# Attention and gated feed-forward on one core: the first pair's queries and first three key blocks come in fp32 by the hardware queues, and GpSimd's cast loads wait for those keys

## The chip, the cores and the metric

The kernel runs on one core of a Trainium2 chip. The metric is the device time of one execution in microseconds (us). The profile is that of one execution; its span is counted from the first to the last instruction.

## The reference

Attention over 8 batches of 8 heads with 1152 positions of 64 elements, in which neighbouring queries are averaged in pairs (1152 queries become 576), and behind it a feed-forward without a nonlinearity: two projections are multiplied element by element, then come two more matrices.

```
q_pool = q.reshape(B, H, S // 2, 2, D).mean(axis=3)
scores = matmul(q_pool, k.T) / sqrt(D)
attn   = softmax(scores)                  # over the 1152 keys
x      = (attn @ v) as [B * 576, 512]     # heads side by side
out    = ((x @ w1) * (x @ w2)) @ w3 @ w_out
```

Inputs and output are fp32; `w1`, `w2` are 512x1024, `w3` 1024x1024, `w_out` 1024x512; the output is 4608x512.

## The kernel before

All matrix work is done in fp16 with fp32 sums. Two heads are one *pair*: there are 32 pairs, and a pair has 9 key blocks of 128 keys. In a pair the two heads' queries lie on the two halves of the 128 partitions once they are transposed.

**Loads.** `load_q`, `load_k` and `load_v` (lines 75 to 97) issue from GpSimd's queue; they read fp32 from memory and write fp16 into the staging tiles `qst`, `kst` and `vst`, so each is a cast load. `load(P)` issues keys, queries and values of a pair. GpSimd also issues the weights (`load_w3`, `load_ffn`, `load_wo`, lines 313 to 331). Lines 430 to 443 write out the order of the first loads by hand: queries of pair 0, its keys in two pieces (blocks 0 to 2, then 3 to 8), the identity for the transposes (`memset` and `affine_select`), values of pair 0, then pair 1, a quarter of `w3`, pair 2, `w_out`, another quarter, pair 3, a third. Later loads are issued from inside the main loop. GpSimd takes them strictly in this order, and at most eight of its DMAs are in flight: the ninth waits for the first to land, through a semaphore that they share.

**The first pair.** `prep_first` (lines 171 to 199) makes the operands of pair 0. ACT copies key blocks 0 to 2 from `kst` to `kc` (line 179). VectorE adds neighbouring queries in two pieces, blocks 0 to 3 and 4 to 8 (line 183; the factor of one half is in the scale of the exponential). TensorE transposes queries (line 189) and keys (line 168) against the identity, VectorE copies the transposed queries to `qT` (line 192), ACT the keys to `kT` (line 197). Key blocks 3 to 8 follow in `prep_rest` (lines 201 to 208), behind the first three chunks of scores. For pairs 1 to 7, VectorE adds the queries (`pool_q`, line 121) and copies the keys (line 164), TensorE transposes both in one group and VectorE takes them out (lines 224 to 232). From pair 8 on GpSimd adds the queries, and the SP queue transposes by DMA (`prep_dma`).

**The main loop** (lines 505 to 562). The scores of all pairs are one stream of chunks of 512 columns. `scores` (line 253) writes a chunk for both heads into a PSUM tile `psc` of three buffers, which the transposes and half of the side work share; `expo` (line 263) takes it through the exponential on ACT into the ring `er`, which holds 9216 columns (18 chunks) for each head. `attend` (line 278) multiplies the ring's columns with the values. How many such products follow in each of the 108 iterations stands in the list `PVS`. Between them TensorE works off a queue of side work: transposing `w3` (line 343), multiplying it with `w_out` into `T16` (line 355), and early feed-forward groups (lines 371 and 389). VectorE empties the PSUM tiles of that work (lines 348, 359, 381, 383) in the program's order, in which its copies for the next pair stand too. What is left of the feed-forward comes after the loop.

**Names that the steps below touch.** `seen` is a tile of one element, which the helper `settled` (line 151) fills on GpSimd with a copy of one element of `kT`, so that GpSimd waits for what wrote it. `ident` is the identity. Each engine runs its instructions in the order in which the program issues them.

Of the kernel before, what the change touches and what calls it, by code (L numbers as in the profile page):

```python
# [7 lines left out]
FP32 = mybir.dt.float32  # L8
# [7 lines left out]
NJ = 9  # L16
PAIR = SQ * NJ
CH = 512
RING = 9216
# [4 lines left out]
def kernel(  # L24
# [11 lines left out]
    nc = tc.nc  # L36
    B, H, S, D = q.shape
# [23 lines left out]
    er = const.tile([128, 2, RING], FP16)  # L61
# [3 lines left out]
    seen = const.tile([1, 1], FP16)  # L65
# [7 lines left out]
    kst, vst, qst, kT, qT, kTs, qTs, qps = {}, {}, {}, {}, {}, {}, {}, {}  # L73

    def load_q(P):
        b, h0 = P // 4, 2 * (P % 4)
        if P % 2 == 0:
            qst[P // 2] = stage.tile([128, 2, 18, D], FP16, tag="qst", bufs=2, name="qst")
        o = 64 * (P % 2)
        nc.gpsimd.dma_start(  # L80
            out=qst[P // 2][o:o + 64].rearrange("p u t d -> p u (t d)"),
            in_=q[b, h0:h0 + 2].rearrange("u (p t) d -> p u (t d)", t=18))

    def load_k(P):
        b, h0 = P // 4, 2 * (P % 4)
        kst[P] = stage.tile([128, 2, NJ, D], FP16, tag="kst", name="kst")
        for js in ((0, 3), (3, NJ)) if P == 0 else ((0, NJ),):
            nc.gpsimd.dma_start(  # L88
                out=kst[P][:, :, js[0]:js[1], :],
                in_=k[b, h0:h0 + 2].rearrange("u (p j) d -> p u j d", j=NJ)[:, :, js[0]:js[1], :])  # L90

    def load_v(P):
        b, h0 = P // 4, 2 * (P % 4)
        vst[P] = stage.tile([128, 2, NJ, D], FP16, tag="vst", name="vst")
        nc.gpsimd.dma_start(  # L95
            out=vst[P].rearrange("p u j d -> p u (j d)"),
            in_=v[b, h0:h0 + 2].rearrange("u (p j) d -> p u (j d)", j=NJ))

    def load(P):
        if P < NP:  # L100
            load_k(P)
            load_q(P)
            load_v(P)

    def load_two(P):
        load_q(P)
        load_q(P + 1)
        load_v(P)
        load_v(P + 1)
        load_k(P)  # L110
        load_k(P + 1)
# [13 lines left out]
    def new_kq(P):  # L125
        if P % 2 == 0:
            kTs[P // 2] = ab.tile([128, 2, NJ, 128], FP16, tag="kT", bufs=2, name="kT")
            qTs[P // 2] = ab.tile([128, NJ, 128], FP16, tag="qT", bufs=2, name="qT")
        o = 64 * (P % 2)
        kT[P] = kTs[P // 2][:, P % 2]  # L130
        qT[P] = qTs[P // 2][:, :, o:o + 64]
# [23 lines left out]
    def new_kc(P):  # L155
        if P % 2 == 0:
            kc2[P // 2] = ab.tile([128, 2, NJ, 2, D], FP16, tag="kc", bufs=1, name="kc")
        kcs[P] = kc2[P // 2][:, P % 2]
        return kcs[P]
# [6 lines left out]
    def keys(P, dst, js):  # L166
        for n, j in enumerate(js):
            nc.tensor.transpose(dst[:, 128 * n:128 * n + 128],
                                kcs[P][:, j].rearrange("p u d -> p (u d)"), ident)

    def prep_first():

        new_kq(0)
        kc = new_kc(0)
        qp = qps[0] = ab.tile([128, NJ, 2, D], FP16, tag="qp", bufs=2, name="qp")
        src = qst[0][0:64].rearrange("p u (c two) d -> p u c two d", two=2)
        tq = psum.tile([128, 2, 1024], FP16, tag="psc", bufs=3, name="tq")
        tk = psum.tile([128, 2, 1024], FP16, tag="psc", bufs=3, name="tk")
        nc.scalar.copy(out=kc[:, 0:3].rearrange("p j u d -> p u j d"), in_=kst[0][:, :, 0:3])
        parts = (range(0, 4), range(4, NJ))  # L180
        for cs in parts:
            r = slice(cs[0], cs[-1] + 1)
            nc.vector.tensor_tensor(
                out=qp[0:64, r].rearrange("p c u d -> p u c d"),
                in0=src[:, :, r, 0, :], in1=src[:, :, r, 1, :], op=ALU.add)
        for h, cs in enumerate(parts):
            for c in cs:
                o = 64 * (c - cs[0])
                nc.tensor.transpose(tq[:, h, o:o + 64],
                                    qp[0:64, c].rearrange("p u d -> p (u d)"),  # L190
                                    ident[0:64, 0:64])
            nc.vector.tensor_copy(
                out=qT[0][:, cs[0]:cs[-1] + 1],
                in_=tq[:, h, 0:64 * len(cs)].rearrange("p (c f) -> p c f", f=64))
            if h == 0:
                keys(0, tk[:, 0], range(0, 3))
                nc.scalar.copy(out=kT[0][:, 0:3].rearrange("p j f -> p (j f)"),
                               in_=tk[:, 0, 0:384])
        return tk
# [162 lines left out]
    def ffn_groups(t):  # L362
# [64 lines left out]
    NIT = NCHUNK // BURST  # L427
    NPV = NP * 90

    load_q(0)  # L430
    load_k(0)
    nc.gpsimd.memset(ident, 0.0)
    nc.gpsimd.affine_select(
        out=ident, in_=ident, compare_op=ALU.not_equal, fill=1.0,
        base=0, channel_multiplier=1, pattern=[[-1, 128]])
    load_v(0)
    load(1)
    load_w3(0)
# [4 lines left out]
    load_w3(2)  # L443
    loaded, staged, prepped, copied = 4, 1, 1, 1
    rest = prep_first()

    n_units = NT // 512
# [41 lines left out]
    for c in range(NF):  # L489
        t = (6, 7, 8, 9, 11, 12, 14, 15)[c]  # L490
# [115 lines left out]
```

## Time and profile before

| | us |
|---|---|
| four runs | 422.08, 422.26, 423.63, 426.41 |
| median | 422.94 |
| profiled execution, whole time | 423.63 |
| its span | 421.9 |
| TensorE (PE) matmuls busy | 404.1 (96% of the span) |
| ScalarE (ACT) busy | 326.3 (77%) |
| VectorE (DVE) busy | 198.0 (47%) |
| GpSimd (POOL) busy | 121.0 (29%) |
| GpSimd's DMA queue | 33.56 MB written, 51.5% of 16 engines' span |
| SP's DMA queue | 24.66 MB, 32.7% |

Lines with `PE` are matmuls and transposes, with `PEld` the loading of their stationary operand. In a timeline line stand: start, length, engine, line of the kernel, operation, tile written and tile read, shapes, count, and in brackets the idle time before with what ended it. A cast load is counted by the bytes that it writes, half of those that it reads. GpSimd is busy while it issues a DMA; the transfer itself runs on the 16 DMA engines.

### The profile page before, as it was taken

How to read it: one execution, taken by the hardware profiler on the slowest of the kernel's cores; microseconds unless marked ns; L12 is line 12 of the kernel's file. 1: busy time of each engine (PE TensorE's matmuls, PEld its weight loads, DVE VectorE, ACT ScalarE, POOL GpSimd, SP SyncE). 2: the span in 40 equal slices, each digit the busy share in tenths (PEclk: the TensorE clock that was granted, in tenths of full speed). 3: DMA queues.
4: the chain of work that ended last, by engine and by line, in shares of the span. 5: the costliest groups of instructions: out<-in, count | busy, mean ns of one | idle time of the engine just before them, and what ended most of it. 6: DMA issues, size and time to landing. Idle time of an engine off the chain costs nothing.

```text
span 421.9 us, 12560 instructions
## 1 busy us (share of the span) xinstructions
PE 404.1 (96%) x5432; PEld 268.2 (64%) x5432; DVE 198.0 (47%) x406; ACT 326.3 (77%) x355; POOL 121.0 (29%) x160
## 2 busy tenths in 40 slices
PE   3998999999999999999999999999999999999995
PEld 1576778666685568665865686667765876544443
DVE  1455655564535543545445535544457434714130
ACT  4899899889888889889888889888888889133332
POOL 8323332253434343423316161524243000000000
PEclk9999999999999999999999999999999999999999
DMA  8999999778989989998989898989899650050404
GB/s 123 202 208 204 180 193 176 122 138 145 156 154 174 184 148 184 170 143 122 165 127 174 148 183 131 206 131 172 164 174 130 113 114 18 13 117 0 102 0 100
DMA packets 94729, 59.15 MB, mean 140 GB/s; under 512 B 65361, under 2 KB 85073, under 8 KB 94673
## 3 DMA queue, kind: packets, MB, share of 16 engines
q0 software_dynamic: 26544, 33.56, 51.5%
q1 hardware_dynamic: 67968, 24.66, 32.7%
q8 instruction: 42, 0.69, 0.7%
q10 hardware_dynamic: 160, 0.13, 0.1%
q14 instruction: 15, 0.11, 0.1%
HBM read 67.11 MB, written 9.44 MB: 181 GB/s over the span
## 4 chain that ended last, share of the span: by engine, by line
PE 79%; DMA 16%; DVE 2%; POOL 1%; issue 1%; ACT 0%; SPq 0%; DVEq 0%; POOLq 0%
PE po L278 18%; PE psc L253 16%; PE pa L371 15%; PE pb L371 15%; PE pp L389 15%; DMA qst<-in_q_dram 7%; DMA w3h<-in_moe_w_dram 4%; DMA w1sb<-in_moe_w_dram 4%; PE pT L355 1%; DMA out_dram<-osb 1%; DVE vt L134 1%; POOL kst L88 1%; DVE gT L383 0%; POOL vst L95 0%; POOL qst L80 0%
## 5 line engine op out<-in xcount | busy, mean ns | idle before, releaser
L263 ACT ACTIVATE er<-psc 128x1024 f16<-128x1024 f32 x324 | 307.7, 1026 | 44.6 <-PE psc L253 44.3
L278 PEld LDWEIGHTS <-er 128*128 128x128 f16 x2880 | 103.9, 98 | 23.7 <-issue 7.0
L278 PE MATMUL po<-vt,er 128*128 128x65 f16 x2880 | 111.3, 194 | 0.7 <-DVE xn L295 0.4
L253 PE MATMUL psc<-qT,kT 64*128 64x512 f16 (+7 forms) x1152 | 97.3, 290 | 6.0 <-ACT er L263 2.8
L383 DVE TENSOR_TENSOR gT<-pb,asb 128x512 f16<-128x512 f32 x72 | 49.8, 692 | 55.8 <-PE pb L371 55.0
L371 PE MATMUL pa<-xT,w1sb 128*128 128x512 f16 x288 | 74.2, 380 | 0.0
L371 PE MATMUL pb<-xT,w2sb 128*128 128x512 f16 x288 | 74.1, 380 | 0.0
L389 PE MATMUL pp<-T,gT 128*128 128x256 f16 (+1 forms) x488 | 67.9, 292 | 0.0
L253 PEld LDWEIGHTS <-kT 64*128 64x128 f16 x1152 | 46.4, 95 | 31.1 <-issue 11.0
L389 PEld LDWEIGHTS <-gT 128*128 128x128 f16 x488 | 45.6, 98 | 18.5 <-issue 3.7
L381 DVE COPY asb<-pa 128x512 f32<-128x512 f32 x56 | 38.7, 691 | 39.0 <-PE pa L371 37.8
L371 PEld LDWEIGHTS <-w2sb 128*128 128x128 f16 x288 | 26.4, 98 | 32.7 <-issue 3.9
L371 PEld LDWEIGHTS <-w1sb 128*128 128x128 f16 x288 | 25.0, 98 | 30.1 <-issue 6.2
L121 POOL TENSOR_TENSOR qp<-qst 128x1152 f16<-128x1152 f16 x12 | 28.5, 2375 | 48.2 <-DMA qst<-in_q_dram 26.4
L401 DVE TENSOR_SCALAR osb<-pp 128x256 f32<-128x256 f32 x49 | 20.8, 425 | 39.3 <-PE pp L389 32.6
L291 DVE RECIPROCAL rz<-po 128x5 f32<-128x5 f32 x64 | 12.4, 193 | 47.2 <-PE po L278 46.7
L295 DVE TENSOR_TENSOR xn<-po,rz 128x320 f16<-128x320 f32 x64 | 31.5, 492 | 2.2
L141 POOL COPY kc<-kst 128x576 int32<-128x576 int32 x24 | 15.9, 666 | 51.3 <-DMA kst<-in_k_dram 51.3
L95 POOL DMA_DIRECT2D vst<-in_v_dram x32 | 23.5, 745 | 13.2 <-DMA kst<-in_k_dram 4.0
L88 POOL DMA_DIRECT2D kst<-in_k_dram x33 | 24.1, 743 | 8.4 <-DVE rz L291 2.6
L398 ACT ACTIVATE osb<-pp 128x512 f32<-128x512 f32 (+1 forms) x12 | 7.0, 579 | 24.2 <-PE pp L389 23.1
L80 POOL DMA_DIRECT2D qst<-in_q_dram x32 | 19.9, 624 | 13.0 <-issue 3.1
(39 smaller groups left out, 127.8 us busy)
## 6 DMA issues: line engine op xcount, KB each, us to landing
qst<-in_q_dram POOLq DMA_DIRECT2D x32, 288.0 KB, 6.5
vst<-in_v_dram POOLq DMA_DIRECT2D x32, 288.0 KB, 10.0
out_dram<-osb SPq DMA_DIRECT2D x70, 128.0 KB, 2.6
kst<-in_k_dram POOLq DMA_DIRECT2D x31, 288.0 KB, 12.3
w3h<-in_moe_w_dram POOLq DMA_DIRECT2D x4, 512.0 KB, 15.8
xT<-in_moe_w_out_dram POOLq DMA_DIRECT2D x2, 512.0 KB, 14.6
w1sb<-in_moe_w_dram POOLq DMA_DIRECT2D x2, 512.0 KB, 16.2
w2sb<-in_moe_w_dram POOLq DMA_DIRECT2D x2, 512.0 KB, 17.7
```

The source lines that it names most:

```text
L88: nc.gpsimd.dma_start(out=kst[P][:, :, js[0]:js[1], :], in_=k[b, h0:h0 + 2].rearrange("u (p j) d -> p u j d", j=NJ)[:, :, js[0]:js[1], :])
L95: nc.gpsimd.dma_start(out=vst[P].rearrange("p u j d -> p u (j d)"), in_=v[b, h0:h0 + 2].rearrange("u (p j) d -> p u (j d)", j=NJ))
L121: eng.tensor_tensor(out=qps[pp][r].rearrange("p c u d -> p u c d"), in0=src[:, :, :, 0, :], in1=src[:, :, :, 1, :], op=ALU.add)
L253: nc.tensor.matmul(t[:, u, o:o + ln].rearrange("p (c f) -> p c f", f=64), kT[P][s, j, :], qT[P][s, f0 // 64:(f0 + ln) // 64], start=True, ...
L263: nc.scalar.activation(out=er[:, :, r:r + CH], in_=psc.pop(c), func=AF.Exp, bias=0.0, scale=SCALE)
L278: nc.tensor.matmul(po[P, u][:, VW * x:VW * x + D + 1], er[:, u, r:r + 128], vts[P % 4][:, u, j, 0:D + 1], start=(m == 0), stop=(m == 44), ...
L295: nc.vector.tensor_tensor(out=xn[:, P % 2, :, u, :], in0=acc[:, :, 0:D], in1=rz.to_broadcast([128, 5, D]), op=ALU.mult)
L371: nc.tensor.matmul(p, w[:, mc, ft * 128:ft * 128 + 128], xT[:, mc, t0:t0 + 512], start=(mc == 0), stop=(mc == NC - 1))
L381: nc.vector.tensor_copy(out=asb[ft], in_=p)
L383: nc.vector.tensor_mul(out=gT[:, ft, :], in0=p, in1=asb.pop(ft))
L389: nc.tensor.matmul(p[:, 0:n], gT[:, ft, 128 * i:128 * i + 128], T16[:, ft, n * s:n * s + n], start=(ft == 0), stop=(ft == NF - 1))
L401: nc.vector.tensor_scalar_mul(out=osb, in0=p[:, 0:n], scalar1=1.0 / (SCL * SCL))
```

## The change

`load_first` issues three DMAs at the program's head: from SP the queries of pair 0, in two pieces (8 and 10 of the 18 consecutive rows that each of 64 partitions holds for a head), and from ACT its key blocks 0 to 2. They are fp32 without a cast, and land in the end of the exponentials' ring `er`, whose columns are seen as fp32 (`q0f`, `k0f`); the ring's end is first written by the exponentials of chunks 9 to 17. `prep_first` reads the queries and keys from there: VectorE's two adds and ACT's copy now have fp32 operands. GpSimd's two cast loads of the same data are gone. Before its first cast load GpSimd now copies one element of the landed keys into `seen`, and so waits for that DMA; the identity is made ahead of this wait. The cast loads of key blocks 3 to 8 of pair 0 and everything behind them follow it. In `load_q` the staging tile is allocated for pair 1, as pair 0 no longer has one.

```diff
     def load_q(P):
         b, h0 = P // 4, 2 * (P % 4)
-        if P % 2 == 0:
+        if P % 2 == 0 or P == 1:
             qst[P // 2] = stage.tile([128, 2, 18, D], FP16, tag="qst", bufs=2, name="qst")
...
-        for js in ((0, 3), (3, NJ)) if P == 0 else ((0, NJ),):
-            nc.gpsimd.dma_start(
-                out=kst[P][:, :, js[0]:js[1], :],
-                in_=k[b, h0:h0 + 2].rearrange("u (p j) d -> p u j d", j=NJ)[:, :, js[0]:js[1], :])
+        j0 = 3 if P == 0 else 0
+        nc.gpsimd.dma_start(
+            out=kst[P][:, :, j0:NJ, :],
+            in_=k[b, h0:h0 + 2].rearrange("u (p j) d -> p u j d", j=NJ)[:, :, j0:NJ, :])
...
+    k0f = er[:, 0, RING - 768:RING].bitcast(FP32).rearrange("p (u j d) -> p u j d", u=2, d=D)
+    q0f = er[0:64, 1, RING - 4608:RING].bitcast(FP32).rearrange("p (u t d) -> p u t d", u=2, d=D)
+
+    def load_first():
+        for ts in (slice(0, 8), slice(8, 18)):
+            nc.sync.dma_start(out=q0f[:, :, ts],
+                              in_=q[0, 0:2].rearrange("u (p t) d -> p u t d", t=18)[:, :, ts])
+        nc.scalar.dma_start(out=k0f,
+                            in_=k[0, 0:2].rearrange("u (p j) d -> p u j d", j=NJ)[:, :, 0:3, :])
+
     def prep_first():
...
-        src = qst[0][0:64].rearrange("p u (c two) d -> p u c two d", two=2)
+        src = q0f.rearrange("p u (c two) d -> p u c two d", two=2)
...
-        nc.scalar.copy(out=kc[:, 0:3].rearrange("p j u d -> p u j d"), in_=kst[0][:, :, 0:3])
+        nc.scalar.copy(out=kc[:, 0:3].rearrange("p j u d -> p u j d"), in_=k0f)
...
-    load_q(0)
-    load_k(0)
+    load_first()
     nc.gpsimd.memset(ident, 0.0)
     nc.gpsimd.affine_select(
         out=ident, in_=ident, compare_op=ALU.not_equal, fill=1.0,
         base=0, channel_multiplier=1, pattern=[[-1, 128]])
+    nc.gpsimd.tensor_copy(out=seen, in_=er[0:1, 0, RING - 768:RING - 767])
+    load_k(0)
     load_v(0)
```

## The prediction, on record before the changed kernel was run

> **What bounds the kernel now.** I read the page's 40 slices first, then the chain of waits cut to the first 86 us, then the timeline around its joints, last the start. In the slices a digit is the busy share in tenths:
>
> ```profile
> PE   3998999999999999999999999999999999999995
> PEclk9999999999999999999999999999999999999999
> DMA  8999999778989989998989898989899650050404
> ```
>
> TensorE is short of work in the first slice (0 to 10.5 us) and at the very end, its clock is never cut, and the DMA engines are full from the start. In five-us stretches TensorE is busy 72.45 of the first 85 us and 331.64 of the last 337. What can be won or lost lies in the first 85 us. There the chain (start, length, what) reads:
>
> ```profile
> 8.12 12.30 DMA qst<-in_q_dram
> ...
> 20.71 16.33 DMA w3h<-in_moe_w_dram
> ...
> 37.33 16.25 DMA w1sb<-in_moe_w_dram
> ...
> 53.87 19.32 DMA qst<-in_q_dram
> ...
> 73.21 0.76 DVE qp L121
> 73.99 0.46 DVE kc L164
> 74.45 0.60 DVE w3T L348
> 75.05 0.34 DVE T L359
> ...
> 75.44 0.40 PE psc L253 x4
> ```
>
> From 8.12 to 73.19 us nothing but GpSimd's cast loads: each lands, frees one of eight slots in flight, the next is issued 0.29 us later. The queue never runs dry (DMA share 1.15 to 1.29 in the stretches 8:20, 20:45, 45:73), so a load lands at the time the stream started plus the bytes ahead of it over the stream's pace. VectorE then takes what landed, in program order, and TensorE waits for a PSUM buffer that VectorE empties behind it. Timeline around 75 us:
>
> ```profile
> 73.21 0.76 DVE L121 TENSOR_TENSOR qp<-qst 64x1152 f16<-64x1152 f16 x1 [2.28 <-DMA qst<-in_q_dram]
> 75.44 0.40 PE L253 MATMUL psc<-qT,kT 64*128 64x128 f16 x4 [0.70 <-DVE T L359]
> ```
>
> The brackets are idle time and its releaser: VectorE 2.28 us for the queries, TensorE 0.70 us for VectorE. The same pair stands at 41.54 (2.38 us) and 43.64 (0.85 us). So TensorE is ahead of the stream, waits for it twice, and is full after that. **The time of the end is the time of the cast stream, plus a constant.**
>
> **The change, part by part.** Sums are made against the profiled execution: 423.63 us, of which 421.9 us span and 1.73 us around it, taken as unchanged. The median of the four runs, 422.94 us, is 0.69 us lower; I add the shift to the median.
>
> *What leaves GpSimd:* two cast loads at its head (queries 0.76 us of issue, three key blocks 0.72 us). They wrote 0.295 + 0.098 = 0.393 MB in fp16 and read twice that. How far the old stream had come by when, from a table by stretches (stretch, length, busy time of five engines, granted clock, DMA share, GB/s written):
>
> ```profile
> 2.60:3.00 0.40, 0.00 (x0) 0.00 (x0) 0.00 (x0) 0.00 (x0) 0.40 (x2) 1.00 1.15 69
> 3.00:3.40 0.40, 0.00 (x0) 0.00 (x0) 0.00 (x0) 0.00 (x0) 0.40 (x1) 1.00 0.66 58
> 3.40:3.80 0.40, 0.00 (x0) 0.00 (x0) 0.00 (x0) 0.00 (x0) 0.33 (x3) 1.00 0.58 104
> 3.80:4.20 0.40, 0.00 (x0) 0.00 (x0) 0.00 (x0) 0.00 (x0) 0.40 (x2) 1.00 1.06 190
> ```
>
> GB/s times 0.4 us, summed on through 213, 160 and 187, gives 0.393 MB at 5.4 us. Bytes start at 2.70 us, 1.45 us after the issue at 1.25; the slow first us costs 2.70 - 0.393/0.19 = 0.63 us against the steady 190 GB/s. So the new stream is level with the old one if its first byte (the other six key blocks) moves at full pace at 5.4 us. Every us later is a us on the end.
>
> *What comes in:* 0.786 MB of fp32 by SP (queries, 262 and 328 KB) and ACT (keys, 196 KB). Both engines are released at 0.74 us; the trace has no hardware load, so I bound it by its nearest row, the 128 KB output stores: 0.58 us of issue each, first bytes about 0.9 us after the issue (issued at 391.85, 26 GB/s in 392.6:393.0), landing after 2.2 us at least and 2.4 in the middle, 205 to 215 GB/s while they run, so 2.4 - 0.9 - 0.6 = 0.9 us from last byte to landing. The cast loads read 410 GB/s (205 written). Fast end: the keys land like an undisturbed store, 0.75 + 2.2 + 0.16 for 64 KB more = 3.1 us. Slow end: they land last of all bytes at the store's pace, 1.65 + 786/215 + 0.9 = 6.2 us. I take 1.65 + (196 + 262)/312 + 0.9 = **4.0 us**: with the keys runs the first query piece, the second is issued 0.58 us later behind it; 312 is the mean of 215 and 410, as loads share the reading side with one row and the uncast form with the other.
>
> Behind those rows, the Trainium skill ("DMA: Bandwidth & Descriptors", Rules for kernel authors) speaks against the change: spreading DMAs over SP, ACT and GpSimd brings no bandwidth, since all run on the same 16 engines. The same page (Anatomy of one DMA) gives 2.0 us plus bytes over 436 GB/s for one cast-queue DMA; an estimate by it for the three together would be 0.75 + 2.0 + 1.8 = 4.55 us, and the sum below would be +1.6 instead of +1.0. No run here shows a hardware load yet.
>
> *The new wait:* GpSimd's copy of one key into `seen` holds back every cast load behind it (six key blocks, values, pair 1, w3, all the rest). Its price is in a later row of the same helper copy: 0.18 us, then 0.28 us before the next issue, 0.46 together. Identity memset and select (0.23 and 0.29 us) move ahead of it and are done by 2 us, under the wait.
>
> *The stream's restart:* 4.0 + 0.46 + 1.45 = 5.91 us to first bytes, 0.51 behind the level point. The slow first us comes again: between none (the old one began with the 64-partition queries) and 0.63; I take 0.5, nearer the only cold start shown. **Stream shift +1.0 us**; ends: 3.1 + 0.46 + 1.45 - 5.4 = -0.4, and 6.2 + 0.46 + 1.45 + 0.63 - 5.4 = +3.3.
>
> *The start of TensorE:* the timeline shows what its first scores, at 7.73 us, follow from:
>
> ```profile
> 1.25 0.76 POOL L80 DMA_DIRECT2D qst<-in_q_dram  x1 [0.80 <-POOLq L590]
> 2.00 1.44 POOL L88 DMA_DIRECT2D kst<-in_k_dram  x2
> ...
> 5.44 0.82 DVE L183 TENSOR_TENSOR qp<-qst 64x512 f16<-64x512 f16 x2 [4.40 <-DMA qst<-in_q_dram]
> 5.86 0.51 ACT L179 COPY kc<-kst 128x384 f16<-128x384 f16 x1 [3.84 <-DMA kst<-in_k_dram]
> ```
>
> New: second query piece lands at 1.65 + 786/312 + 0.9 = 5.1. VectorE's two adds read fp32: by the rows 692 ns (512 elements) and 492 ns (320) that is 0.69 and 0.83 us for 418 and 476 ns, +0.63. Second add 5.1 to 5.9, five transposes 0.44, copy 0.33, scores at 6.75: 1.0 us earlier (2.0 to 0 between the ends). It costs nothing and brings nothing: pair 1's queries land at 13.05 + 1.0, and TensorE then waits for them (it reached that point at 14.95, the add took 0.76); at 20.42 VectorE took queries 0.06 us after they landed, so from there on TensorE runs about 1 us late.
>
> *Hidden:* ACT's issue (0.5 us) ahead of its 1.28 us table load ends at 2.5 us, before the keys. ACT's cast from fp32 is at most the 0.59 us of a 128x512 fp32 copy for 0.51. Keys 3 to 8: issue 4.46 plus the old 4.5 us landing is 9.0, copy 0.35, six transposes 0.82, copy 0.56: 10.7, where the old ended at 11.5; cover is gone when they land after 9.7. Exponentials wait for the old contents of the ring, long read. SP's first transposes come at 27.21, so its two issues block nothing. Three more hardware DMAs turn the eight semaphores on; each wait is for a DMA eight back. With two cast loads fewer, GpSimd's first wait for a free slot moves two loads on; slots set when a load is issued, its place in the queue sets when it lands.
>
> Sum: 422.94 + 1.0 = **423.9 us** (424.6 against the profiled execution's own 423.63).
>
> **The rivals.**
> - *The keys land fast* (faster side). At the undisturbed 3.1 us, and without a slow start, the shift is -0.4 and the time 422.5 us. For it: the DMA engines stand idle before 2.7 us. Against: three loads share them. It decides below a landing of 3.5 us (3.5 + 0.46 + 1.45 = 5.4).
> - *The keys land last.* Short rows (768 bytes) against 2 KB ones, queries into 64 partitions, store pace: 6.2 us, shift +3.3, 426.2 us. For it: stores of 64 partitions ran at 215 GB/s with the engines 0.9 busy.
> - *The start gain survives.* If TensorE were not tied to the stream, 1.0 us earlier scores would give 421.9 us. Against: the waits at 43.64 and 75.44 and the chain above. For it: TensorE's waits are only 0.85 and 0.70 us.
>
> **How the numbers follow.** Forecast 0.55, keys last 0.2, keys fast 0.15, start gain survives 0.1. The forecast's own range is 423.2 to 424.9 (keys at 3.6 to 4.8 us and slow start 0.2 to 0.6). For 8 in 10 I reach to the first two rivals' times, and 0.4 below the first for the scatter of a median: 422.1 to 426.2; the third and part of the second stay out. About 1% (4.2 us) is what a measurement here can tell from no change; the four runs spread over 422.08 to 426.41. No case gives -4.2 us: faster 0.01. Only the slow end with something added passes +4.2: slower 0.04. Within 1%: 0.95.
>
> **What would show it.** Right: keys copied on ACT near 4.0 us; a hole in the DMA's GB/s between about 4.5 and 5.9; first scores near 6.75; every cast load from pair 1 on landing about 1 us later (13.05 to 14, 20.42 to 21.4, 73.19 to 74.2); VectorE still waiting at the queries near 42 and 74; the chain still all DMA to 74. Wrong: queries landing at 73 or earlier, a TensorE without the 0.70 us wait at 75, or a hole so long that ACT waits for keys 3 to 8.

## The result, and the profile after

The changed kernel takes 1.0028 times the time of the kernel before, with a 95% interval of 1.0003 to 1.0052: some 1.2 us more, between 0.1 and 2.2. That lies where the forecast put it (423.9 for 422.94, +1.0), but not for the reason that the forecast gave. The medians over all executions are 426.44 us (35) and 423.22 us (56), 3.2 us apart; of these, executions more than 1.5% above the fastest of their kernel (11 and 6) are left out of the ratios, and of the means and counts over several runs below. The profiled execution of the changed kernel took 431.9 us (span 430.1): its start is read here, where it agrees with the later profiles, and its end only to see where time can be lost.

The start in the timeline after:

```profile
0.74 1.44 SPq L176 DMA_DIRECT2D er<-in_q_dram  x2
0.74 0.45 ACTq L178 DMA_DIRECT2D er<-in_k_dram  x1
...
3.45 0.51 ACT L189 CAST kc<-er 128x384 f16<-128x384 f32 x1 [0.94 <-DMA er<-in_k_dram]
3.48 0.18 POOL L445 COPY seen<-er 1x1 f16<-1x1 f16 x1 [2.17 <-DMA er<-in_k_dram]
3.60 0.88 POOL L88 DMA_DIRECT2D kst<-in_k_dram  x1
...
4.63 0.68 DVE L193 TENSOR_TENSOR qp<-er 64x512 f16<-64x512 f32 x1 [3.59 <-DMA er<-in_q_dram]
...
6.11 0.82 DVE L193 TENSOR_TENSOR qp<-er 64x640 f16<-64x640 f32 x1 [0.79 <-DMA er<-in_q_dram]
...
8.02 1.04 PE L263 MATMUL psc<-qT,kT 64*128 64x512 f16 x6 [0.42 <-DVE qT L202]
...
13.05 0.76 DVE L121 TENSOR_TENSOR qp<-qst 64x1152 f16<-64x1152 f16 x1 [0.84 <-DMA qst<-in_q_dram]
```

The keys are there at 3.45 us (5.86 before), and GpSimd issues its first cast load 0.15 us later. But the first scores wait for the *queries*: the two pieces land at 4.6 and 6.1 us, VectorE's adds take 0.68 and 0.82 us (0.82 together before), and the first scores start at 8.02 us, 0.29 later than before. Pair 1's queries are taken at 13.05 us, as before. Stretches around the restart (columns as in the prediction; the last is GB/s):

```profile
2.50:3.00 0.50, 0.00 (x0) 0.00 (x0) 0.00 (x0) 0.01 (x1) 0.00 (x0) 1.00 1.05 348
3.00:3.50 0.50, 0.00 (x0) 0.00 (x0) 0.00 (x0) 0.05 (x1) 0.02 (x1) 1.00 1.24 359
...
4.50:5.00 0.50, 0.00 (x0) 0.00 (x0) 0.36 (x1) 0.00 (x0) 0.50 (x1) 1.00 0.84 210
5.00:5.50 0.50, 0.12 (x3) 0.13 (x4) 0.32 (x1) 0.00 (x0) 0.50 (x2) 1.00 0.75 56
5.50:6.00 0.50, 0.50 (x7) 0.34 (x6) 0.00 (x0) 0.00 (x0) 0.50 (x2) 1.00 0.62 51
6.00:6.50 0.50, 0.20 (x2) 0.00 (x0) 0.39 (x1) 0.26 (x1) 0.50 (x2) 1.00 1.12 166
```

Some 350 GB/s while keys and queries run together, 210 to 225 once only the queries do (from 4 to 5 us), then the hole and the slow first us of the cast stream.

A second profile of the changed kernel (e1, span 421.5 us) answers to the page and the chain. Its slices:

```profile
PE   2988999999999999999999999999999999999996
PEclk9999999999999999999999999999999999999999
DMA  8999999698989999997979898979799641050404
```

They look as before. The chain of waits, cut to 86 us (its longest pieces), does not:

```profile
1.54 4.75 DMA er<-in_q_dram
6.31 0.82 DVE qp L193
8.22 0.62 PE psc L263 x2
8.93 1.03 ACT er L273
...
12.59 2.86 ACT er L273 x3
...
71.09 0.80 PE psc L263 x10
72.44 1.94 ACT er L273 x2
...
77.88 1.85 PE pT L365 x16
```

Before, it was cast loads from 8 to 73 us. Now it starts with the hardware load of the queries and then goes almost wholly through TensorE and ACT. At the place where VectorE waited 2.28 us for queries and TensorE 0.70 us for VectorE, e1 has:

```profile
71.35 0.76 DVE L121 TENSOR_TENSOR qp<-qst 64x1152 f16<-64x1152 f16 x1 [0.34 <-DMA qst<-in_q_dram]
```

VectorE's wait at this place is 0 to 1.57 us in the other five profiles of this start, but in none of the six is a wait of TensorE for VectorE's `T` or `w3T` left between 20 and 85 us.

### The profile page after: what moved, and what is told of

It reads as the page before. It is cut to its first block, busy times and chain, and to the rows that moved or that the text cites. A ratio compares the mean times of both kernels' runs of the same rounds, so it can differ in the third digit from the quotient of the medians.

```text
span 430.1 us, 12569 instructions
## 1 busy us (share of the span) xinstructions
PE 406.3 (94%) x5432; PEld 269.2 (63%) x5432; DVE 196.3 (46%) x406; ACT 326.4 (76%) x355; POOL 120.3 (28%) x159
## 4 chain that ended last, share of the span: by engine, by line
DMA 45%; PE 37%; ACT 6%; POOL 6%; issue 2%; SPq 1%; DVE 1%; POOLq 0%; ACTq 0%; DVEq 0%
DMA kst<-in_k_dram 26%; DMA kT<-kc 11%; PE psc L263 7%; PE po L288 7%; PE pb L381 7%; PE pa L381 6%; ACT er L273 6%; PE pp L399 6%; DMA qst<-in_q_dram 3%; PE pT L365 3%; DMA out_dram<-osb 3%; POOL qst L80 2%; POOL kc L141 2%; POOL vst L95 1%; DMA qT<-qp 1%
```

## The experiments

All twelve were timed beside the kernel before; e5 is a single execution. The marks below are read from each one's timeline: first scores; the scores behind key blocks 3 to 8 ("fourth"); the sixteen `T` products near 78 us; the time between these two; GpSimd's query adds for pair 8 and pair 30, the first and last but one turn of the loop of loads; and TensorE's waits behind 85 us. The marks of e7 stand with it.

| kernel | first scores | fourth | T products | between | pair 8 | pair 30 | waits |
|---|---|---|---|---|---|---|---|
| before | 7.73 | 11.54 | 78.44 | 66.90 | 81.78 | 317.62 | 0.3 |
| before again, e5 | 7.79 | 11.60 | 77.77 | 66.17 | 80.68 | 316.29 | 0.2 |
| before, five osb, e10 | 7.81 | 11.62 | 77.97 | 66.35 | 80.91 | 310.25 | 0 |
| changed | 8.02 | 11.90 | 77.70 | 65.80 | 81.15 | 321.44 | 7.4 |
| changed again, e1 | 8.22 | 12.10 | 77.81 | 65.71 | 80.04 | 317.43 | 0.9 |
| changed again, e9 | 8.03 | 11.91 | 77.96 | 66.05 | 81.50 | 318.80 | 1.0 |
| changed, five osb, e8 | 8.01 | 11.89 | 77.69 | 65.80 | 79.41 | 317.49 | 1.2 |
| changed, five osb, e12 | 8.28 | 12.16 | 78.07 | 65.91 | 80.14 | 317.36 | 0.2 |
| wait for queries, e2 | 8.09 | 13.13 | 80.88 | 67.75 | 84.29 | 323.77 | 2.8 |
| no wait, e3 | 9.60 | 13.48 | 79.28 | 65.80 | 79.79 | 319.48 | 0.4 |
| keys only, e4 | 8.62 | 12.50 | 78.30 | 65.80 | 79.53 | 317.71 | 1.0 |
| keys only again, e6 | 7.82 | 11.70 | 77.50 | 65.80 | 79.64 | 309.95 | 0 |
| keys only, five osb, e11 | 9.32 | 13.20 | 79.00 | 65.80 | 78.68 | 317.10 | 0 |

**e1: the changed kernel again.** No edit.

> The changed kernel once more. In its profile the keys landed at 3.45 us, GpSimd's next cast load was issued at 3.60, pair 1's queries landed at 13.05 as before, and the first scores came at 8.02 us for 7.73. Theory S (the start): in a run without stalls the end moves by that start alone, so the lowest time is 0.3 us above the lowest of before (some 422.0 for 421.7), and the median moves more only through stalls behind 85 us. Theory C (the cast stream sets the end): the stream is level or 0.6 us early, so the lowest and the median would be 0 to 0.6 us below before. Chance: the stalls behind 85 us come as often as in the kernel before, and the medians are then 0.3 us apart.

Ratio 1.0014 (0.9971 to 1.0056), median 425.34 us of 12, lowest 422.62; the kernel before beside it 423.65 of 29, lowest 421.77. The interval holds every theory. The median stands 1.7 us above, more than the start's 0.3 us, and the stream theory's gain does not show.

**e2: GpSimd waits for the second query piece.**

```diff
-    nc.gpsimd.tensor_copy(out=seen, in_=er[0:1, 0, RING - 768:RING - 767])
+    nc.gpsimd.tensor_copy(out=seen, in_=er[0:1, 1, RING - 1:RING])
```

> GpSimd waits for the second query piece (landed at 6.1 us) in place of the keys (3.45). The stream starts 2.6 us later. Theory C: pair 1's queries land at 15.6, the queries of the chain near 75.5, and the time is 2.0 to 2.6 us above that of the changed kernel. Theory S: TensorE's first scores stay at 8.0; but key blocks 3 to 8 land near 10.7 for 8.0 and hold up the fourth chunk by some 1.5 us, all behind goes with it, and the time is 0.5 to 1.5 us above.

Ratio 1.0103 (1.0045 to 1.0161), median 428.92 us. The first cast load is issued at 6.99 us for e1's 3.84, 3.15 later. The timeline:

```profile
6.21 0.84 POOL L445 COPY seen<-er 1x1 f16<-1x1 f16 x1 [4.90 <-DMA er<-in_q_dram]
...
10.86 0.66 DVE L212 COPY kc<-kst 128x768 f16<-128x768 f16 x1 [2.83 <-DMA kst<-in_k_dram]
...
17.97 0.76 DVE L121 TENSOR_TENSOR qp<-qst 64x1152 f16<-64x1152 f16 x1 [4.31 <-DMA qst<-in_q_dram]
...
18.78 0.66 PE L228 MATMUL t<-ident,qp 64*128 64x64 f16 x9 [1.65 <-DVE qp L121]
```

Key blocks 3 to 8 come late, then pair 1's queries, and TensorE stands for both. Its `T` products are 3.07 us later than e1's, which is the stream's 3.15 almost to the digit: a *late* stream is passed on in full. All of it comes from these first two waits: the seventeen products with the values that e1 starts at 23.24 us start here at 26.39, and from there on TensorE keeps e1's pace. The whole time rose by more (some 3.8 us against e1, by the ratios), with 2.8 us of waits behind 85 us, and behind one of them TensorE ran at a lower clock (see e8); neither theory had that part.

**e3: no wait.** The line with the copy into `seen` is left out.

> GpSimd's copy into seen is left out, so that the cast loads start at about 1.3 us, beside the three hardware loads. Theory C: the stream starts 2.3 us earlier and is at most 1 us ahead behind the hardware loads, and the time falls by 0.5 to 1 us. Theory S: queries and keys share the engines with the cast loads, the second query piece lands at 6.5 to 7.5 in place of 6.1, first scores at 8.4 to 9.4, and the time rises by 0.4 to 1.4 us in runs without stalls.

Ratio 1.0000 (0.9958 to 1.0041), median 424.24 us, lowest 423.14. GpSimd issues at 1.44 us, beside the hardware loads:

```profile
1.44 0.86 POOL L88 DMA_DIRECT2D kst<-in_k_dram  x1
...
7.69 0.82 DVE L193 TENSOR_TENSOR qp<-er 64x640 f16<-64x640 f32 x1 [2.39 <-DMA er<-in_q_dram]
...
9.60 1.04 PE L263 MATMUL psc<-qT,kT 64*128 64x512 f16 x6 [0.42 <-DVE qT L202]
```

The second query piece lands 1.4 to 1.6 us later, first scores come at 9.60 us, and the `T` products follow 65.80 us behind the fourth chunk. VectorE waits for queries nowhere up to 73 us. So an *early* stream is worth nothing on its own: here the start is what TensorE is paced by up to the `T` products, which come 1.5 us later than e1's. On this side the start theory has the marks right. The whole time does not show it: the lowest of twelve is 0.5 us above e1's, the median 1.1 us below, and the means are not told apart (-0.7 us, -2.1 to +0.8). So what the wait is worth in the whole time is not shown.

**e4 and e6: keys only.** The queries are GpSimd's first cast load again, and nothing waits.

```diff
-        for ts in (slice(0, 8), slice(8, 18)):
-            nc.sync.dma_start(out=q0f[:, :, ts],
-                              in_=q[0, 0:2].rearrange("u (p t) d -> p u t d", t=18)[:, :, ts])
...
+    load_q(0)
+    load_k(0)
     nc.gpsimd.memset(ident, 0.0)
...
-    nc.gpsimd.tensor_copy(out=seen, in_=er[0:1, 0, RING - 768:RING - 767])
-    load_k(0)
```

> Only the three key blocks come by ACT's hardware queue; the queries are GpSimd's first cast load again, as before, and nothing waits. Keys land near 3.2 us, queries near 5.2 (5.44 before), as 196 KB leave the cast stream. Theory S: first scores at 7.4 to 7.6 for 7.73, and the lowest time is 0.2 us below before. Theory C: the stream is 0.5 us earlier behind it, so the time falls by 0.5 us. If the two agree on faster, the marks at 13, 41 and 73 us tell which: Theory C has the loads land 0.5 us earlier.

> The kernel of e4 once more (keys by ACT's queue, queries by the cast queue, no wait). In e4's profile the queries landed at 6.53 us and first scores came at 8.62, later than in the kernel before, and yet its times were the lowest. Theory S: this profile's queries were late by chance; in most runs they land at 5.2 to 5.6, and a second profile shows first scores at 7.3 to 7.8 or a time above 422.3. Theory L (the loop of loads behind 80 us): its stream is 1.5 to 2 us ahead of the changed kernel's, so pair 8's query add comes at 79.5 and TensorE is held up less often behind it: seven or more of twelve times below 422.6 again.

Ratios 0.9976 (0.9931 to 1.0021) and 0.9993 (0.9958 to 1.0028), medians 422.16 and 422.08 us, lowest 421.63 and 421.31; neither interval tells it from the kernel before. Against the changed kernel beside it (e1) the difference is clear: e4's mean is 2.1 us lower (0.5 to 3.7). Fourteen of the 24 times lie at or below 422.2 us; in e6 eight of twelve are below 422.6 and pair 8's add comes at 79.64, as theory L had it, but the loop of loads behind it took 238.2 us in e4 and 230.3 in e6. The queries land at 6.53 us in e4, at 5.72 in e6, at 7.23 in e11:

```profile
3.18 0.51 ACT L186 CAST kc<-er 128x384 f16<-128x384 f32 x1 [0.67 <-DMA er<-in_k_dram]
...
5.72 0.82 DVE L190 TENSOR_TENSOR qp<-qst 64x512 f16<-64x512 f16 x2 [4.68 <-DMA qst<-in_q_dram]
```

(that is e6). So this landing varies by 1.5 us between executions. All three have the same 65.80 us between the fourth chunk and the `T` products, and never a wait for the stream.

**e5: the kernel before, once more.** No edit, one profiled execution.

> The kernel before, unchanged, for a second look at its marks: first scores (7.73 us in the first profile), the fourth chunk's scores behind key blocks 3 to 8 (11.54), the sixteen T products near 78.4 us, pair 8's query add on GpSimd (81.78), pair 30's (317.62). Theory S (start) says that the end is the fourth chunk's scores plus some 65.8 us to the T products plus some 342.5 us, as long as no wait for the stream or the loop comes in between: from e1, e3 and e4 that is 65.7 to 65.8 and 342 to 343. Here it should be the same within 0.5 us, plus TensorE's waits behind 85 us that the profile names.

422.51 us, span 420.7. First scores and fourth chunk within 0.06 us of the first profile, but no wait of 0.85 us at 43 or 0.70 at 75: TensorE's waits for VectorE behind the stream, on which the forecast was built, belonged to that one execution:

```profile
71.63 0.76 DVE L121 TENSOR_TENSOR qp<-qst 64x1152 f16<-64x1152 f16 x1 [0.66 <-DMA qst<-in_q_dram]
```

What stays is 66.17 us between the two marks instead of 65.80, and no wait for the stream is in it. The eight transposes of `w3` at 19 us take 1.03 us (0.83 in e6), the products behind them 1.19 (0.71), and ACT waits for scores:

```profile
19.20 1.03 PE L343 MATMUL w3t<-ident,w3h 128*128 128x128 f16 x8
...
21.58 8.56 ACT L263 ACTIVATE er<-psc 128x1024 f16<-128x1024 f32 x9 [0.27 <-PE psc L253]
```

e10, with 66.35 us, has the same (1.04 us, ACT's wait 0.43), and so has the changed kernel in e9, with 66.05 (1.04 us, wait 0.16). Eight such transposes at 22 us take 0.61 us in all of them; why TensorE is slower up to some 20 us, and not equally long, no run here shows.

**e7: the loop's own wait left out.** In `prep_dma`'s turn:

```diff
-                settled(prepped)
```

> The changed kernel without the helper settled in the main loop: GpSimd issues the next two pairs' loads without waiting until the transposes of the pair before have landed (4.8 us of wait in each of eleven turns). Theory L: the loop's turn falls from 21.5 us to under 20, TensorE never waits for it, the times draw together at 422.0 to 422.8, and the median falls by 2 us or more against the changed kernel's 425.3. Rival: the loads now run beside the DMA transposes, which take longer than their 4.8 us, and TensorE waits for keys: median unchanged or above.

Ratio 1.0235 (1.0207 to 1.0263). The rival holds, though the loop itself turns faster (225.2 us from pair 8 to pair 30 for e1's 237.4). The transposes of keys and queries land after 10.0 and 11.0 us (median of 12) where e1's take 5.1 and 3.7, and the first one makes TensorE wait:

```profile
102.42 1.47 PE L263 MATMUL psc<-qT,kT 64*128 64x512 f16 x10 [9.14 <-DMA qT<-qp]
```

It is the only wait behind 85 us that the profile names, and within it TensorE's granted clock falls to 0.50, where it stays until 105 us. Here, keeping cast loads away from the transposes is worth far more than the wait costs. Up to 78 us this kernel is the changed one (fourth chunk 12.13, `T` products 77.93).

**e8 and e12: the changed kernel with five output buffers; e10: the kernel before with five; e11: keys only with five.**

```diff
-                    osbs[i] = ffp.tile([128, dm], FP32, tag="osb", bufs=3, name="osb")
+                    osbs[i] = ffp.tile([128, dm], FP32, tag="osb", bufs=5, name="osb")
```

> The changed kernel with five output buffers osb for three. In its first profile TensorE lost 6.9 us behind 85 us to VectorE's output copy L411, which waited for output stores that stand behind the transposes on SP's queue. If the stores' place in that queue is what turns a late loop into TensorE's wait, two more buffers take most of it away: median 422.3 to 423.5 for 425.3, and the lowest stays at 422.0 to 422.6. Rival: the loop is late for TensorE itself (keys of the next pairs), the wait then shows at the scores as a wait for kT or qT, and the median stays at 425.

> The kernel before with five output buffers for three. With the stalls behind 85 us gone (as in e8), what is left is the start: lowest at 421.7, median 422.0 to 422.6. Against the changed kernel with five (e12) the start theory has it 0.3 to 0.5 us lower. The stream theory, in which the changed kernel's stream is level or ahead and TensorE waits 0.4 to 1.5 us for it here, has it 0 to 1 us higher.

> Keys alone by the hardware queue (e4), with five output buffers. By the start theory first scores stand level with the kernel before (7.82 in e6), and the stream 0.9 us ahead takes away TensorE's waits at 41 and 73 us: lowest 421.3 to 421.7, median 421.6 to 422.2, 0.3 to 0.6 us below the kernel before with five buffers and below both kernels as they are.

> The changed kernel with five output buffers again (e8), beside the kernel before with five. Start theory: lowest 422.0 to 422.2, median 0.3 to 0.5 us above that of e10. If the whole 1.2 us of the measured change is in the start or the stream and not in the stalls, it stays 1.2 us above.

They start from what the changed kernel's first, longest profile shows behind 85 us:

```profile
248.93 3.96 SPq L420 DMA_DIRECT2D out_dram<-osb  x4
```

```profile
254.76 0.42 DVE L411 TENSOR_SCALAR osb<-pp 128x256 f32<-128x256 f32 x1 [0.15 <-PE pp L399]
259.69 0.42 DVE L411 TENSOR_SCALAR osb<-pp 128x256 f32<-128x256 f32 x1 [4.50 <-DMA out_dram<-osb]
```

```profile
260.17 0.40 PE L263 MATMUL psc<-qT,kT 64*128 64x320 f16 x4 [3.73 <-DVE osb L411]
```

SP issues four output stores behind its transposes; they land after 8.6 to 10.0 us instead of 2.6 (the median in e1), VectorE has no output buffer, and TensorE no PSUM tile. Of the nine profiles with three buffers and the loop's own wait five have such a wait of TensorE, of the four with five buffers none. The rival is there too, but smaller: 0.5 us of the first profile's waits and 1.0 us of e9's are for `qT`.

Such a wait can cost more than its own length. Behind another one of the first profile, TensorE's granted clock falls to half of full speed (the column before the last two):

```profile
308.15 0.39 PE L263 MATMUL psc<-qT,kT 64*128 64x128 f16 x4 [2.42 <-DVE osb L411]
```

```profile
310.00:311.00 1.00, 1.00 (x4) 0.33 (x3) 0.25 (x1) 0.00 (x0) 0.00 (x0) 0.50 1.03 198
311.00:312.00 1.00, 1.00 (x20) 1.00 (x19) 0.69 (x1) 0.00 (x0) 0.00 (x0) 0.50 1.12 217
```

From 309 to 313 us the clock is 0.72, 0.50, 0.50 and 0.58, in sum 1.7 us of TensorE's time; four products of `pb` take 1.82 us there for 1.03 at 314.58. With 6.5 us more of waits than in e1 that makes some 8 of the 8.6 us by which this span is longer. In e2 the clock falls the same way behind a wait of 2.03 us at 261.10, again 1.7 us; with the later `T` products (3.07) and 1.9 us more of waits that makes 6.7 for the 6.6 us measured between its span and e1's. The wait of 3.73 us at 260.17 is followed by no such fall; what decides is not shown. The clock makes long executions longer, but it does not part the two kernels: among executions whose mean granted clock is 0.997 or more, the changed kernel's 37 lie 1.0 us above 64 of the kernel before (0.4 to 1.7).

With five buffers the medians are 423.01 (e8) and 423.31 us (e12) for the changed kernel's 425.34 (e1) and 426.13 (e9), and 422.67 (e10) for the kernel before. In the mean the two buffers take 1.5 us off the changed kernel (0.8 to 2.2) and 1.0 us off the kernel before (0.2 to 1.7). The difference between changed and before with five buffers is +0.6 us in the mean, interval -0.2 to +1.4: told neither from none nor from the 1.1 us with three buffers (e9). The medians of e12 and e10 are 0.64 us apart, between the two cases of e12's expectation. e11 (422.71) brings nothing more; in its profile the queries landed late, at 7.23 us.

**e9: the changed kernel a third time.** No edit.

> The changed kernel a third time, for the share of its runs that stall behind 85 us. So far 27 of 47 runs lay above 424.9 us, against 35 of 108 of the kernel before. If the change makes the loop of loads late more often, it is again half or more of twelve, with a median above 424.5; if that share was chance, it is three to five of twelve and the median is 423.2 to 424.

Ratio 1.0026 (0.9978 to 1.0073), median 426.13 us of 12, seven of them above 424.9: the first case of the expectation. With e1 and the first result, 20 of 45 executions of the changed kernel lie above 424.9 us and 33 of 127 of the kernel before; their means differ by 1.1 us (0.4 to 1.7).

## Why the prediction was right, and where it was not

*Keys at 4.0 us.* They landed at 3.43 to 3.69 in six profiles. Inside the bounds (3.1 to 6.2); the rate while keys ran was some 350 GB/s, not the 312 taken.

*0.46 us from keys to the next issue.* 0.15 to 0.16: the 0.28 us gap of the later row does not come here.

*Restart.* First cast bytes some 1.5 us after the issue and a slow first us, as taken. With the keys measured, the working would have given a shift of some +0.2 us. Pair 1's queries are taken at 13.36 us in the mean of six profiles for 13.10 of three: +0.3. Near 41 and 72 us nothing is left of it. **The term that failed is "stream shift +1.0".** By its own signs the prediction was wrong in its mechanism: the queries were taken at 73 us or earlier (70.92 to 72.70), and TensorE's 0.70 us wait at 75 was gone.

*First scores 1.0 us earlier.* They came 0.2 to 0.55 us *later*. The adds were sized right (0.69 and 0.83 for 0.68 and 0.82). The second piece landed at 6.10 to 6.37 for 5.1: a rate of 312 or more was there only while the keys ran beside; queries into 64 partitions alone ran at 210 to 240, near the slow bound, and landing came 0.9 us behind the last bytes. Another 0.3 us was not in the sum: VectorE's copy of the first four transposes (0.28 us) now stands behind the second add, and the last five transposes wait for it.

*"The time of the end is the time of the cast stream, plus a constant".* Half of it stands. e2 shows it for a late stream, us for us. e3, e4, e6 and e11 show what lies below it: the work of TensorE and ACT takes some 65.8 us from the fourth chunk to the `T` products when nothing waits for the stream. The kernel before stands at 66.2 to 66.9 there, the changed one at 65.7 to 66.1. So at the `T` products both are level (78.06 in the mean of three profiles, 77.86 of six): the change gives 0.4 us at the start and gets back 0.6 us between the marks. Only in the first profile of the kernel before are these waits for the stream (1.1 us); the 0.4 and 0.55 us of e5 and e10 come from the slower products near 20 us, which e9 shows as well. *Start gain survives* was a rival with its sign the wrong way: there was no gain, and the loss did not survive either.

*"Plus a constant" behind 75 us.* Wrong, and here, as both kernels are level at the `T` products, is where the measured time must be. The loop from pair 8 to pair 30, in which GpSimd's loads, its copies and SP's transposes wait for each other, took 235.8 and 235.6 us in the kernel before, 237.4 and 237.3 in the changed one (e1, e9), and with five buffers 229.3 and 238.1 and 237.2. A long loop can become a wait of TensorE: e8 shows one way in which it does, as two more output buffers take most of the high times away, from both kernels. It need not: e3 has a loop of 239.7 us and e11 one of 238.4, with 0.4 us of waits and none.

**What stays open** is why the loop is long more often in the changed kernel. TensorE, VectorE and SP run the same instructions in the same order there, pair 8's add starts no later in the mean (80.3 us for 81.1), and yet four of four profiles (237.2 to 238.1, the first one left out) lie above three of three of the kernel before (229.3 to 235.8). Keys only had 230.3, 238.2 and 238.4 in three profiles of the same start, so the loop's length differs between executions of one kernel by 8 us, and seven profiles do not settle it. From the `T` products to the end of the span these four take 343.0 to 343.9 us, the kernel before 342.2 to 343.5, and e3 with its longer loop 342.5. The prediction has the three new DMAs turn the eight semaphores on, so that later DMAs share them differently; no run varied that alone. That the times differ by some 1 us is shown; that the loop's length carries it is argued from these profiles, not shown by an experiment.

So the time was right by luck: a stream delay of 1.0 us that did not come, and about as much lost behind the `T` products, which was not in the sum and whose cause stays open. In the Trainium skill ("DMA: Bandwidth & Descriptors", Rules for kernel authors) it says that DMAs spread over several issuers gain no bandwidth; e3 agrees as far as it goes: the second query piece landed some 1.5 us later beside cast loads.

## What to carry to other kernels

When two chains, a start and a stream of loads, meet in one engine, take the waits between them from more than one execution: those in a single profile may be that execution's own. Before moving a load for its latency, ask which operand lands last; keys 2.4 us earlier brought nothing, as the queries came 0.7 us later. And look behind the stretch that you edit: here a loop of loads beside the compute scattered by 8 us between executions, while edits of the start moved the `T` products by 3 us at most, and two more buffers at the place where the loop meets the compute took 1.0 to 1.5 us off the mean.

## What was not expected of the hardware

- Hardware loads of 128 and 64 partitions together ran at some 350 GB/s, those of 64 partitions alone at 210 to 240. From issue to landing 2.7 us for 192 KB of keys, 3.9 and 4.5 us for the query pieces beside them.
- DMA transposes beside cast loads take two to three times as long to land (10.0 us for 5.1 and 11.0 for 3.7, e7).
- A wait of TensorE of 2.0 to 2.4 us was twice followed by some 3.4 us at a granted clock of 0.50 (first profile and e2), a wait of 3.7 us once by none.
- The same cast load of 288 KB at the program's head landed at 5.7 to 7.2 us from one execution to the next when a hardware load ran beside it (e4, e6, e11), and at 5.44 to 5.53 in three profiles without.
